# Warm-up matmuls, the spacing of the first block's bursts, and the place of one convolution in a tuned conv + SwiGLU kernel

## The chip, the cores and the metric

The kernel runs on one core of a Trainium2 chip. The metric is the device time of one execution in microseconds (us). "Span" is the time from the first to the last instruction of the profiled execution; in these runs it is 1.7 to 1.9 us shorter than the device time.

## The reference

```python
# x (8, 4096, 192), weight (8, 7); w_gate, w_val (192, 1536), w_out (1536, 192)
w   = softmax(weight)                       # seven taps for each of eight heads of 24 columns
y   = causal_conv_over_sequence(x, w)       # y[s] = sum_k w[h, k] * x[s - 6 + k]
y   = y.reshape(32768, 192)
out = (silu(y @ w_gate) * (y @ w_val)) @ w_out
```

## The kernel before

Tokens are worked through in 64 blocks of 512; a block has twelve *steps*. A step `n` computes one chunk of 128 hidden features: six matmuls of 512 columns for gate and value (`gate_val`), a silu on ScalarE, a product on VectorE. The down projection of the chunks is done in *bursts* of 12 or 24 matmuls (`slot(1)` to `slot(4)` for each block). Four blocks make a unit.

The convolution is done on TensorE too. For most units its result takes a detour ("the hop"): out to DRAM scratch and back through transposing DMAs. The first four blocks do not have time for all of that (in the kernel before, the first hop's writes and transposes are issued from 47.3 to 67.2 us, and the first gate matmul comes at 9.01 us): `early(e)` does their conv, and blocks 0 to 2 are turned by TensorE (`eturn`). The program divides PSUM into three "gate" banks, three "val" banks and two accumulators, which `eturn` and the conv borrow.

```python
    def keep_warm(count, width=TB):                      # TB = 512, P = 128
        for _ in range(count):
            seq(nc.tensor.matmul(warm[:, 0:width], fill[:, 0:P], fill[:, 0:width], ...))

    acc_banks = (apool, "acc0"), (apool, "acc1")
    keep_warm(7)
    spread_taps()          # two tiny matmuls, two VectorE operations
    keep_warm(5, P)
    make_wide()            # four matmuls of 256 columns, then copies out of PSUM
    early(0, (gate_bank, gate_bank, val_bank))
    eturn(0, (*acc_banks, gate_bank))
    make_band()

    for n in range(n_steps):
        b, j = divmod(n, NCH)                            # NCH = 12
        u, ls = divmod(n, ustep)                         # ustep = 48
        work = None
        if n in (11, 19):
            def work(e=2 if n == 11 else 3):
                early(e, (gate_bank, gate_bank, val_bank))
        at = (28, 31) if u == 0 else (10, 22)
        if u + 1 < NU and ls in at:
            def work(u=u, hh=at.index(ls)):
                conv_half(u + 1, hh)
        gate_val(n)
        if n == 5:
            early(1, (*acc_banks, gate_bank))
        elif n == 7:
            eturn(1, (*acc_banks, gate_bank))
        elif n in (9, 11):
            slot(1 if n == 9 else 2, b, silu[n - 1], work)
        elif n == 13:
            slot(3, 0, silu[n - 1])
        elif j % 3 == 1 and b:
            k = {1: 3, 4: 4, 7: 1, 10: 2}[j]
            slot(k, b - 1 if j < 7 else b, silu[n - 2], work if j > 4 else None)
            if j == 4 and work:
                work()
        if n == 18:
            eturn(2, (*acc_banks, gate_bank))
        # ... cut: writing out and fetching conv results, loads and copies of x
```

The third argument of `slot` is a silu that the burst must wait for. Bursts alternate which half of the array's rows adds into which accumulator, and the program takes the silu of a step as the sign that the burst before it has drained.

Of the kernel before, what the change touches and what calls it, by code (L numbers as in the profile page):

```python
# [10 lines left out]
def kernel(  # L11
# [9 lines left out]
    nc = tc.nc  # L21
    fp32 = mybir.dt.float32
    fp16 = mybir.dt.float16
# [11 lines left out]
    P = 128  # L35
# [4 lines left out]
    TB = P * SUBS  # L40
# [31 lines left out]
    def seq(i):  # L72

        e = i.ins.engine
        if e in last_on:
            tc.add_manual_dep(i.ins, last_on[e].name, NOSYNC, reason="order")
        last_on[e] = i.ins
        return i

    wpool = ctx.enter_context(tc.tile_pool(name="wts", bufs=1))  # L80
# [6 lines left out]

    wraw = wpool.tile([H, K], fp32, tag="wraw", name="wraw")
    seq(nc.sync.dma_start(out=wraw, in_=weight))
    fill = wpool.tile([P, TB], fp16, tag="fill", name="fill")  # L90
    seq(nc.vector.memset(fill, 0.0))  # L91


# [188 lines left out]
    def spread_taps():  # L282
        bank = apool.tile([P, TB], fp32, tag="acc0", name="tapbank")
        for a in range(2):
            seq(
                nc.tensor.matmul(
                    bank[:, a * H : a * H + H],
                    split[:, a].rearrange("h k q -> h (k q)"),
                    eye[0:H, 0:H],
                    start=(a == 0),  # L290
                    stop=True,
                    skip_group_check=True,
                )
            )
        seq(nc.vector.tensor_copy(tap, bank[:, 0 : 2 * H]))
        seq(
            nc.vector.tensor_tensor(
                spread.rearrange("p j a h -> p j (a h)"),
                eyes,
                tap.unsqueeze(1).to_broadcast([P, 16, 2 * H]),  # L300
                op=ALU.mult,
            )
        )
# [118 lines left out]
    def eturn(b, where):  # L422
        xc[b] = []
        for k in range(SL):
            t = cpool.tile([P, XW], fp16, tag=f"xc{k}", name=f"xc{k}", bufs=6)
            pool, tag = where[k]
            bank = pool.tile([P, EG, P], fp16, tag=tag, name="turn")
            for g in range(EG):
                seq(
                    nc.tensor.transpose(  # L430
                        bank[:, g, :], tme[b][:, g, Q * k : Q * k + P], ident
                    )
                )
            seq(
                (dve, act, dve)[k](
                    t.rearrange("p (g c j) -> p g c j", c=2, j=EO),
                    bank.rearrange("p g (c q) -> p g c q", c=2)[:, :, :, 0:EO],
                )
            )
            xc[b].append(t)  # L440
# [86 lines left out]
    silu = {}  # L527
# [26 lines left out]
    def down(b, work, swap, after):  # L554
        first = True
        for second, js in work:
            for j in js:
                hj = hbuf[b * NCH + j]
                for s in range(2):
                    for half in range(2):  # L560
                        bank = half ^ swap
                        p0 = Q * half
                        i = seq(
                            nc.tensor.matmul(  # L564
                                acc[b][bank][:, s, :],
                                hj[p0 : p0 + Q, ts(2 * bank + s, P)],
                                wo16[p0 : p0 + Q, j, :],
                                start=(not second and j == 0 and s == 0),
                                stop=(second and j == NCH - 1),
                                skip_group_check=True,  # L570
                            )
                        )
                        if first and after is not None:
                            tc.add_manual_dep(
                                i.ins, after.name, SYNC, reason="row halves swap banks"
                            )
                        first = False
                if second:
                    del hbuf[b * NCH + j]
# [15 lines left out]
    G = [range(3 * q, 3 * q + 3) for q in range(4)]  # L595

    def slot(k, b, after=None, between=None):

        if k == 1:
            acc[b] = [  # L600
                apool.tile([P, 2, D], fp32, tag=f"acc{i}", name=f"acc{i}")
                for i in range(2)
            ]
            down(b, [(False, G[0])], 1, after)
            if between is not None:
                between()
            down(b, [(False, G[1])], 1, None)
        elif k == 2:
            down(b, [(True, G[0]), (True, G[1])], 0, after)
            if between is not None:  # L610
                between()
            if b < n_blocks - 1:
                down(b, [(False, G[2])], 0, None)
        elif k == 3:
            down(b, [(True, G[2]), (False, G[3])], 1, after)
        else:
            down(b, [(True, G[3])], 0, after)
            o_sb = hpool.tile([P, SUBS, D], fp32, tag="o_sb", name="o_sb", bufs=3)
            seq(nc.scalar.copy(o_sb[:, 0:2, :], acc[b][0]))  # L619
            seq(nc.vector.tensor_copy(o_sb[:, 2:4, :], acc[b][1]))  # L620
            t0 = b * TB
            seq(
                nc.sync.dma_start(
                    out=out[t0 : t0 + TB, :].rearrange("(s p) d -> p s d", p=P),
                    in_=o_sb,
                )
            )
            del acc[b]


    warm = ppool.tile([P, TB], fp32, tag="gate", name="warm")

    def keep_warm(count, width=TB):
        for _ in range(count):
            seq(
                nc.tensor.matmul(  # L636
                    warm[:, 0:width], fill[:, 0:P], fill[:, 0:width],
                    start=True, stop=True, skip_group_check=True,
                )
            )  # L640

    gate_bank, val_bank = (ppool, "gate"), (ppool, "val")
    acc_banks = (apool, "acc0"), (apool, "acc1")
    keep_warm(7)
    spread_taps()
    keep_warm(5, P)
    make_wide()
    early(0, (gate_bank, gate_bank, val_bank))
    eturn(0, (*acc_banks, gate_bank))
# [3 lines left out]
    for n in range(n_steps):  # L653
        b, j = divmod(n, NCH)
        u, ls = divmod(n, ustep)
        work = None
        if n in (11, 19):

            def work(e=2 if n == 11 else 3):
                early(e, (gate_bank, gate_bank, val_bank))  # L660

        at = (28, 31) if u == 0 else (10, 22)
        if u + 1 < NU and ls in at:

            def work(u=u, hh=at.index(ls)):
# [4 lines that stand above are left out]
            early(1, (*acc_banks, gate_bank))  # L670
        elif n == 7:
            eturn(1, (*acc_banks, gate_bank))
        elif n in (9, 11):
            slot(1 if n == 9 else 2, b, silu[n - 1], work)
        elif n == 13:
            slot(3, 0, silu[n - 1])
        elif j % 3 == 1 and b:
            k = {1: 3, 4: 4, 7: 1, 10: 2}[j]
            slot(k, b - 1 if j < 7 else b, silu[n - 2], work if j > 4 else None)
            if j == 4 and work:  # L680
                work()
        if n == 18:
            eturn(2, (*acc_banks, gate_bank))
        elif n == 20:
            eout(3)
        elif n == 21:
            efetch(3)
        if u + 1 < NU:
            if ls == at[0]:
                conv_dup(u + 1)  # L690
            if ls == at[1]:
                for m in range(2):
                    conv_out(u + 1, m)
            if ls == at[1] + 1:
                for m in range(2, 8):
                    conv_out(u + 1, m)
            lo = 32 if u == 0 else 28
            if ls in range(lo, lo + 12, 3):
                fetch(UB * (u + 1) + (ls - lo) // 3)
        if u + 2 < NU:  # L700
            if ls == (22 if u == 0 else 1):
                x16_tile(u + 2)
                load_x(u + 2, 0, silu[n - 1])
            if ls == (25 if u == 0 else 5):
                load_x(u + 2, 1, silu[n - 1])
            if ls == (29 if u == 0 else 26):
                dup_x(u + 2)
    b = n_blocks - 1
    o_sb = hpool.tile([P, SUBS, D], fp32, tag="o_sb", name="o_sb", bufs=3)
    o_rows = out[b * TB : b * TB + TB, :].rearrange("(s p) d -> p s d", p=P)  # L710
# [5 lines left out]
    seq(nc.sync.dma_start(out=o_rows[:, 0:2, :], in_=o_sb[:, 0:2, :]))  # L716
    down_rows(b, 1, range(9, NCH))
    seq(nc.scalar.copy(o_sb[:, 2:4, :], acc[b][1]))  # L718
    seq(nc.scalar.dma_start(out=o_rows[:, 2:4, :], in_=o_sb[:, 2:4, :]))


# [28 lines left out]
```

## Time and profile before

| | before |
|---|---|
| device time, median of the first 3 runs | 793.12 us (792.34 to 794.83) |
| span of the profiled run | 790.9 us |
| TensorE busy | 783.5 us (99%) |
| VectorE, ScalarE busy | 582.9 us (74%), 522.1 us (66%) |
| chain that ended last | 97% TensorE |

From the page of the kernel before, the busy time of each engine and the chain that ended last, by engine:

```profile
PE 783.5 (99%) x12007; PEld 526.7 (67%) x12007; DVE 582.9 (74%) x928; ACT 522.1 (66%) x910; POOL 67.6 (9%) x95
...
PE 97%; POOL 1%; DMA 1%; DVE 0%; ACT 0%; issue 0%; POOLq 0%
```

TensorE is the limit, and in the long middle it has no gap (from 80 to 140 us it is busy for 60.0 of 60.0 us). So only the first 45 us and the last 5 can change. The timeline of TensorE in the kernel before, start of the kernel; the columns are start in us, duration in us, engine, line, operation, result and operands, shape and count, and in brackets the idle time before it with what ended it:

```profile
1.20 3.17 PE L636 MATMUL warm<-fill 128*128 128x512 f16 x7 [1.20 <-DVE fill L91]
4.31 0.21 PE L286 MATMUL tapbank<-eye,split 8*128 8x8 f16 x2
4.45 0.71 PE L636 MATMUL warm<-fill 128*128 128x128 f16 x5
5.11 1.01 PE L317 MATMUL taps<-spread,shift 128*128 128x256 f16 x4
6.68 0.82 PE L372 MATMUL cv<-xe,wide 64*64 64x72 f16 x64 [0.56 <-ACT wide L330]
8.01 1.04 PE L430 MATMUL turn<-ident,tme 128*128 128x128 f16 x15 [0.50 <-ACT tme L390]
```

Seven warm-ups begin at 1.20 us, and start every 0.427 us; later, matmuls of the same width start every 0.215 us. The trace records full clock from 6.21 us on. The rest is a chain with two pauses of 0.5 us. The first gate matmul follows at 9.01 us.

The same timeline at the last pair of step 9 and the first burst, which follows it, and around the first conv of unit 1 (step 28):

```profile
17.91 0.38 PE L538 MATMUL gate<-xc,w 64*128 64x512 f16 x1
17.91 0.38 PE L538 MATMUL val<-xc,w 64*128 64x512 f16 x1
18.32 1.16 PE L564 MATMUL acc<-wo,h 64*128 64x192 f16 x24
...
41.27 0.66 PE L564 MATMUL acc<-wo,h 64*128 64x192 f16 x12
41.86 0.73 PE L461 MATMUL cv<-x,band 64*32 64x240 f16 x32
42.52 0.40 PE L538 MATMUL gate<-xc,w 64*128 64x512 f16 x1
42.84 0.37 PE L538 MATMUL val<-xc,w 64*128 64x512 f16 x1
...
43.31 0.38 PE L538 MATMUL gate<-xc,w 64*128 64x512 f16 x1
43.87 0.37 PE L538 MATMUL val<-xc,w 64*128 64x512 f16 x1 [0.19 <-DVE tm L478]
```

Gate and value matmuls run as pairs, one in each half of the array, 0.215 us apart from pair to pair. The burst should start 0.21 us after the last pair and starts 0.41 us after it: a hidden wait of 0.2 us that no bracket shows, since a matmul's modelled end covers it (the records are 0.38 us long and start 0.215 us apart). After the conv the value matmuls fall 0.3 to 0.6 us behind their gates, because VectorE has not yet emptied the banks that the conv borrowed ("tm").

### The profile page before, as it was taken

How to read it: one execution, taken by the hardware profiler on the slowest of the kernel's cores; microseconds unless marked ns; L12 is line 12 of the kernel's file. 1: busy time of each engine (PE TensorE's matmuls, PEld its weight loads, DVE VectorE, ACT ScalarE, POOL GpSimd, SP SyncE). 2: the span in 40 equal slices, each digit the busy share in tenths (PEclk: the TensorE clock that was granted, in tenths of full speed). 3: DMA queues.
4: the chain of work that ended last, by engine and by line, in shares of the span. 5: the costliest groups of instructions: out<-in, count | busy, mean ns of one | idle time of the engine just before them, and what ended most of it. 6: DMA issues, size and time to landing. Idle time of an engine off the chain costs nothing.

```text
span 790.9 us, 28567 instructions
## 1 busy us (share of the span) xinstructions
PE 783.5 (99%) x12007; PEld 526.7 (67%) x12007; DVE 582.9 (74%) x928; ACT 522.1 (66%) x910; POOL 67.6 (9%) x95
## 2 busy tenths in 40 slices
PE   8999999999999999999999999999999999999997
PEld 5666666666666666666666666666666666666665
DVE  7677777777777777768777777777777777777775
ACT  6666666666666666766667666666667667676664
POOL 8101010010100101001010000100001010000000
PEclk9999999999999999999999999999999999999999
DMA  9999565787747778467894857857477784726211
GB/s 139 151 199 152 125 116 115 157 121 151 125 104 143 131 145 135 104 133 118 158 138 113 121 112 164 126 143 130 94 149 127 150 120 111 134 80 121 75 42 42
DMA packets 213825, 99.22 MB, mean 125 GB/s; under 512 B 147256, under 2 KB 212800, under 8 KB 212800
## 3 DMA queue, kind: packets, MB, share of 16 engines
q1 hardware_dynamic: 167424, 78.75, 47.4%
q0 software_dynamic: 46000, 18.45, 20.6%
q8 instruction: 94, 1.54, 0.8%
q14 instruction: 35, 0.29, 0.1%
q10 hardware_dynamic: 272, 0.20, 0.1%
HBM read 36.89 MB, written 41.16 MB: 99 GB/s over the span
## 4 chain that ended last, share of the span: by engine, by line
PE 97%; POOL 1%; DMA 1%; DVE 0%; ACT 0%; issue 0%; POOLq 0%
PE gate L538 61%; PE acc L564 32%; PE cv L461 2%; PE val L538 1%; DMA xe<-in_x_dram 1%; POOL w L167 0%; POOL xe L97 0%; PE acc L585 0%; PE cv L372 0%; PE turn L430 0%; DVE h L549 0%; ACT sig L547 0%; DVE tm L478 0%; ACT o_sb L718 0%; DVE o_sb L620 0%
## 5 line engine op out<-in xcount | busy, mean ns | idle before, releaser
L549 DVE TENSOR_TENSOR h<-sig,val 128x512 f16<-128x512 f16 x768 | 507.6, 688 | 195.8 <-PE val L538 194.3
L547 ACT ACTIVATE sig<-gate 128x512 f16<-128x512 f32 x768 | 458.6, 597 | 235.1 <-PE val L538 208.8
L538 PE MATMUL val<-xc,w 64*128 64x512 f16 x2304 | 539.2, 376 | 0.2 <-DVE tm L478 0.2
L538 PE MATMUL gate<-xc,w 64*128 64x512 f16 x2304 | 539.3, 376 | 0.0
L538 PEld LDWEIGHTS <-w 64*128 64x128 f16 x4608 | 254.0, 110 | 183.9 <-issue 1.6
L564 PEld LDWEIGHTS <-h 64*128 64x128 f16 x6096 | 257.4, 94 | 62.8 <-issue 6.1
L564 PE MATMUL acc<-wo,h 64*128 64x192 f16 x6096 | 298.8, 243 | 0.1
L97 POOL DMA_DIRECT2D x<-in_x_dram x40 | 31.5, 792 | 436.3 <-ACT sig L547 427.6
L478 ACT CAST tm<-cv 128x480 f16<-128x480 f32 x60 | 30.6, 562 | 22.0 <-PE cv L461 22.0
L478 DVE CAST tm<-cv 128x480 f16<-128x480 f32 x60 | 36.7, 653 | 2.6
L620 DVE COPY o_sb<-acc 128x384 f32<-128x384 f32 x63 | 34.7, 550 | 0.0
L489 POOL COPY tm<-tm 128x1280 f16<-128x1280 f16 x15 | 18.8, 1254 | 137.0 <-DVE tm L478 116.0
L619 ACT COPY o_sb<-acc 128x384 f32<-128x384 f32 x63 | 30.2, 480 | 0.0
L461 PE MATMUL cv<-x,band 64*32 64x240 f16 x960 | 18.2, 265 | 0.0
L461 PEld LDWEIGHTS <-band 64*32 64x32 f16 x960 | 10.1, 91 | 4.9 <-issue 4.7
L132 POOL MEMSET x<- 6x192 f16 x7 | 1.7, 248 | 59.7 <-PE cv L461 59.6
L97 POOL DMA_DIRECT2D xe<-in_x_dram x9 | 5.9, 672 | 0.8 <-DMA xe<-in_x_dram 0.6
L636 PE MATMUL warm<-fill 128*128 128x512 f16 (+1 forms) x12 | 3.9, 496 | 1.2 <-DVE fill L91 1.2
L390 ACT CAST tme<-cv 128x288 f16<-128x288 f32 x8 | 2.9, 401 | 2.6 <-PE cv L372 2.6
L372 PEld LDWEIGHTS <-wide 64*64 64x64 f16 x256 | 2.7, 108 | 2.0 <-ACT wide L330 1.0
L372 PE MATMUL cv<-xe,wide 64*64 64x72 f16 (+1 forms) x256 | 3.2, 192 | 0.7 <-ACT wide L330 0.6
L430 PE MATMUL turn<-ident,tme 128*128 128x128 f16 x45 | 3.1, 220 | 0.5 <-ACT tme L390 0.5
(52 smaller groups left out, 37.7 us busy)
## 6 DMA issues: line engine op xcount, KB each, us to landing
out_dram<-o_sb SPq DMA_DIRECT2D x63, 384.0 KB
scr<-tm SPq DMA_DIRECT2D x105, 130.0 KB
x<-x SPq DMA_DIRECT2D x28, 480.0 KB
x<-in_x_dram POOLq DMA_DIRECT2D x24, 480.0 KB, 9.0
x<-in_x_dram POOLq DMA_DIRECT2D x7, 468.0 KB, 7.1
xc<-scr SPq DMA_TRANSPOSE x180
scr<-tm SPq DMA_DIRECT2D x15, 104.0 KB
w<-in_moe_w_gate_dram POOLq DMA_DIRECT2D x3, 192.0 KB, 5.3
```

The lines of the kernel that those rows point to most:

```text
L97: nc.gpsimd.dma_start(out=t[p0 + i0 : p0 + i1, w0 - at : w1 - at, :], in_=bass.AP(tensor=x_flat.tensor, offset=(t0 + size * w0 - pad + i0) ...
L372: nc.tensor.matmul(o[Q * c : Q * c + Q, at : at + w], wide[Q * r : Q * r + Q, a, h, :], xe[e][Q * r : Q * r + Q, c : 2 * G : 2, h * grp : ...
L461: nc.tensor.matmul(banks[r][32 * c : 32 * c + 32, t * w : t * w + w], band[Q * r : Q * r + Q, h, :], x16[u][Q * r : Q * r + Q, NG * c : NG ...
L478: eng(tm[u][:, NG * r : NG * r + NG, 2 * grp * hp : 2 * grp * hp + 2 * grp].rearrange("p g (t e) -> p g t e", t=2), banks[r][:, 0 : 2 * w] ...
L489: seq(nc.gpsimd.tensor_copy(tm[u][:, :, SL * Q : 4 * Q], tm[u][:, :, 0:Q]))
L538: nc.tensor.matmul(o, w16[m][p0 : p0 + Q, k, e::E], xc[b][k][p0 : p0 + Q, 0:TB], start=(k == 0), stop=(k == SL - 1),)
L547: silu[n] = seq(nc.scalar.activation(sg, g, AF.Silu)).ins
L549: seq(nc.vector.tensor_tensor(hj, sg, v, op=ALU.mult))
L564: nc.tensor.matmul(acc[b][bank][:, s, :], hj[p0 : p0 + Q, ts(2 * bank + s, P)], wo16[p0 : p0 + Q, j, :], start=(not second and j == 0 and ...
L619: seq(nc.scalar.copy(o_sb[:, 0:2, :], acc[b][0]))
L620: seq(nc.vector.tensor_copy(o_sb[:, 2:4, :], acc[b][1]))
L636: nc.tensor.matmul(warm[:, 0:width], fill[:, 0:P], fill[:, 0:width], start=True, stop=True, skip_group_check=True,)
```

## The change

Its intent: keep TensorE busy from the first instruction until the taps, so that its clock rises early; give block 0's bursts the spacing of all later ones; put the first conv inside a burst, so that the banks it used are emptied during the rest of that burst; and move the copies of x out of the way of the hop. The diff, cut to its core:

```diff
-    fill = wpool.tile([P, TB], fp16, tag="fill", name="fill")
+    fill = wpool.tile([P, P], fp16, tag="fill", name="fill")
@@ slot, k == 3
-            down(b, [(True, G[2]), (False, G[3])], 1, after)
+            down(b, [(True, G[2])], 1, after)
+            if between is not None:
+                between()
+            down(b, [(False, G[3])], 1, None)
@@ start
-                    warm[:, 0:width], fill[:, 0:P], fill[:, 0:width],
+                    warm[:, 0:width], fill,
+                    fill.unsqueeze(1).to_broadcast([P, width // P, P]),
-    keep_warm(7)
+    keep_warm(8)
     spread_taps()
-    keep_warm(5, P)
+    keep_warm(4, 2 * P)
@@ steps
-        if n in (11, 19):
+        if n in (12, 19):                      # conv of block 2, of block 3
-        at = (28, 31) if u == 0 else (10, 22)
+        at = (25, 31) if u == 0 else (10, 22)
-        elif n in (9, 11):
-            slot(1 if n == 9 else 2, b, silu[n - 1], work)
-        elif n == 13:
-            slot(3, 0, silu[n - 1])
-        elif j % 3 == 1 and b:
+        elif n in (9, 12, 15, 17):
+            k = {9: 1, 12: 2, 15: 3, 17: 4}[n]
+            slot(k, 0, silu[n - 1 if k == 4 else n - 2], work)
+        elif j % 3 == 1 and n > 18:
-            slot(k, b - 1 if j < 7 else b, silu[n - 2], work if j > 4 else None)
-            if j == 4 and work:
-                work()
+            slot(k, b - 1 if j < 7 else b, silu[n - 2], work)
@@ loads and copies of x for unit 2 (steps 22, 25 and 29 become 21, 23 and 37)
-            if ls == (29 if u == 0 else 26):
+            if ls == (37 if u == 0 else 26):
                 dup_x(u + 2)
@@ last store
-    seq(nc.scalar.dma_start(out=o_rows[:, 2:4, :], in_=o_sb[:, 2:4, :]))
+    seq(nc.sync.dma_start(out=o_rows[:, 2:4, :], in_=o_sb[:, 2:4, :]))
```

More of the change, by code (lines that the diff above doesn't have):

```diff
@@ L656, with work @@
         work = None
-        if n in (11, 19):
-            def work(e=2 if n == 11 else 3):
+        if n in (12, 19):
+            def work(e=2 if n == 12 else 3):
                 early(e, (gate_bank, gate_bank, val_bank))
-        at = (28, 31) if u == 0 else (10, 22)
+        at = (25, 31) if u == 0 else (10, 22)
         if u + 1 < NU and ls in at:
@@ L700 @@
         if u + 2 < NU:
-            if ls == (22 if u == 0 else 1):
+            if ls == (21 if u == 0 else 1):
                 x16_tile(u + 2)
                 load_x(u + 2, 0, silu[n - 1])
-            if ls == (25 if u == 0 else 5):
+            if ls == (23 if u == 0 else 5):
                 load_x(u + 2, 1, silu[n - 1])
-            if ls == (29 if u == 0 else 26):
+            if ls == (37 if u == 0 else 26):
                 dup_x(u + 2)
```

## The prediction

> **What bounds the kernel now.** TensorE. The page has PE busy 783.5 of 790.9 us (99%), and the chain that ended last is 97% PE. From about 50 to 784 us the matmul timeline shows no idle time: a step of gate and value takes 0.645 us, twelve down matmuls 0.50. The change leaves those blocks alone, so only the 8 us before the first gate matmul, some stalls before 45 us and the 3.6 us after the last copy are in reach. ScalarE (66%) and VectorE (74%) have slack.
>
> **What it moves, costed from the matmul timeline.**
> 1. Down bursts of block 0. At 17.91, 20.41 and 24.17 us the burst starts 0.415 us after the last pair instead of 0.212: it waits for the silu of the step just before. Three steps apart and waiting for the silu two steps back, bursts 1 to 3 lose that: -0.6 us. Burst 4 moves from step 16 to 17 and waits for the step just before: +0.2. It now stands one step ahead of the transposes of block 2, which write the accumulator banks that its copies must empty. Before, VectorE's copy ended 1.5 us after the burst; the second transposes would now come about 1.1 us after it: +0.3 us stall.
> 2. First conv burst. At the end of a down burst, it makes gate/value wait for evacuation: pairs split at 42.52 to 43.88 us, and three steps take 2.47 us instead of 1.94. Inside a burst (as at 45.75 us) this vanishes: -0.5 us. x, issued by 19.3 us with at most 13.8 us to landing, is in time.
> 3. Start. Warm-up matmuls of 512 columns come every 427 ns, so the array is at half clock until about 6 us. [...] If the clock is released as late as in this trace, the extra matmul and the wider second group delay the taps (5.11 us) by 0.3 to 0.6 us. [...] On average -0.3 us.
> 4. Tail. ScalarE's store took about 2.2 us to land, SyncE's half 1.7: -0.2 us at most.
> 5. Copies of x later, loads slightly earlier: off the critical path, 0.
>
> Sum about -1.1 us, 0.14%.
>
> **Prediction.** 792.0 us, range 790.6 to 793.4. Faster by over 2%: 0.003; within 2%: 0.994; slower by over 2%: 0.003.
>
> **What would show each step.** Burst gaps of 0.21 us at steps 9, 12, 15, one of 0.41 at step 17; a pause of some 0.3 us within the transposes of step 18; no PE wait on "tm" after the first conv; warm-up spacing falling from 427 to 213 ns before the taps, and the first gate matmul at 8.2 to 9.3 us (now 9.01); steps from 50 us on unchanged; the end sooner after the last copy.
>
> **What would make it wrong.** [...]three runs span 2.5 us. Transfers of x colliding with unit 1's fetches so that PE waits for xc at step 48. A longer chain of bank waits around steps 17 to 19.

The terms of the forecast come to -0.1 (bursts), -0.5 (first conv), -0.3 (start) and -0.2 us (tail), together -1.1 us. "Phase" of the clock, where the recorded texts below use the word, is the time of its release, which differs from run to run: 4.76 to 6.21 us in six traces with the old start.

## The result, and the profile after

The changed kernel took 791.79 us (median of 4 runs, 791.17 to 793.09), the kernel before 793.04 us beside it (4 runs). The ratio is 0.9983, with a 95% interval of 0.9962 to 1.0004. Such a ratio is the mean time of one kernel's runs over that of the other's of the same rounds, so it is not quite the ratio of the medians. The predicted time of 792.0 us was 0.2 us off. The interval includes 1, so these eight runs alone do not show a gain; what was gained is read from the traces below.

From the page of the changed kernel, the busy times:

```profile
PE 782.5 (99%) x12007; PEld 526.3 (67%) x12007; DVE 583.0 (74%) x928; ACT 522.1 (66%) x910; POOL 67.6 (9%) x95
```

The timeline of TensorE in the changed kernel: the start, the conv of block 1, the burst of step 9, the burst of step 17 with the transposes of step 18, and the first conv of unit 1, now in step 25:

```profile
1.00 3.28 PE L639 MATMUL warm<-fill 128*128 128x512 f16 x8 [1.00 <-DVE fill L91]
4.22 0.20 PE L286 MATMUL tapbank<-eye,split 8*128 8x8 f16 x2
...
5.01 0.60 PE L317 MATMUL taps<-spread,shift 128*128 128x256 f16 x4
...
8.50 0.37 PE L538 MATMUL gate<-xc,w 64*128 64x512 f16 x1
...
12.75 0.38 PE L538 MATMUL val<-xc,w 64*128 64x512 f16 x1
13.56 1.03 PE L372 MATMUL cv<-xe,wide 64*64 64x72 f16 x64 [0.43 <-DMA xe<-in_x_dram]
14.52 0.40 PE L538 MATMUL gate<-xc,w 64*128 64x512 f16 x1
...
17.99 0.38 PE L538 MATMUL val<-xc,w 64*128 64x512 f16 x1
18.20 1.15 PE L564 MATMUL acc<-wo,h 64*128 64x192 f16 x24
...
27.41 0.38 PE L538 MATMUL val<-xc,w 64*128 64x512 f16 x1
27.82 0.67 PE L564 MATMUL acc<-wo,h 64*128 64x192 f16 x12
...
29.07 1.30 PE L430 MATMUL turn<-ident,tme 128*128 128x128 f16 x15
...
38.11 0.66 PE L564 MATMUL acc<-wo,h 64*128 64x192 f16 x12
38.70 0.73 PE L461 MATMUL cv<-x,band 64*32 64x240 f16 x32
39.36 0.67 PE L564 MATMUL acc<-wo,h 64*128 64x192 f16 x12
39.86 0.38 PE L538 MATMUL gate<-xc,w 64*128 64x512 f16 x1
39.86 0.38 PE L538 MATMUL val<-xc,w 64*128 64x512 f16 x1
```

Four things are to be seen. The burst of step 9 now starts 0.21 us after its last pair (17.99 to 18.20 us; the same at steps 12 and 15), and that of step 17 0.41 us after its own. In this run the clock rose early (at 3.84 us; the four matmuls for the taps take 0.60 us, not 1.01), and the first gate matmul came 0.5 us sooner. But the conv of block 1 then waited for the transfer of its x ("xe"), so that step 6, which begins right after it, began at 14.52 us against 14.44 before: this run kept nothing of its better start. The transposes of step 18 take 1.30 us where those of block 0 take 1.04: the new stall. And after the conv the gate and value matmuls stay together.

The last copy and the last store of the kernel before, from its timeline of ScalarE:

```profile
786.26 0.48 ACT L718 COPY o_sb<-acc 128x384 f32<-128x384 f32 x1 [1.65 <-PE acc L585]
786.77 0.41 ACTq L719 DMA_DIRECT2D out_dram<-o_sb  x1
```

The same in the changed kernel, where SyncE issues the store:

```profile
785.46 0.48 ACT L719 COPY o_sb<-acc 128x384 f32<-128x384 f32 x1 [1.65 <-PE acc L585]
786.05 0.39 SPq L720 DMA_DIRECT2D out_dram<-o_sb  x1
```

The traces allow an account by stretches between the same matmuls. "First gate of step n" is the start of that step's first gate matmul.

| stretch | before | after | difference |
|---|---|---|---|
| start to first gate of step 6 | 14.437 | 14.521 | +0.08 |
| to first gate of step 19 (bursts of block 0) | 15.918 | 15.784 | -0.13 |
| to step 23 (burst of step 19) | 6.045 | 5.861 | -0.18 |
| to step 48 (first conv of unit 1) | 26.198 | 25.633 | -0.57 |
| to ScalarE's last copy | 723.667 | 723.665 | 0 |
| last copy to the end of the span | 4.604 | 4.263 | -0.34 |

The sum is -1.14 us, the difference of the spans (790.869 and 789.727 us).

### The profile page after: what moved, and what is told of

Read it like the earlier page. It is cut to its first block, busy times and chain, and to the rows that moved or that the text cites. A ratio compares the mean times of both kernels' runs of the same rounds, so it can differ in the third digit from the quotient of the medians.

```text
span 789.7 us, 28564 instructions
## 1 busy us (share of the span) xinstructions
PE 782.5 (99%) x12007; PEld 526.3 (67%) x12007; DVE 583.0 (74%) x928; ACT 522.1 (66%) x910; POOL 67.6 (9%) x95
## 4 chain that ended last, share of the span: by engine, by line
PE 97%; POOL 1%; DMA 1%; DVE 0%; ACT 0%; issue 0%; POOLq 0%
PE gate L538 61%; PE acc L564 32%; PE cv L461 2%; PE val L538 1%; DMA xe<-in_x_dram 1%; POOL w L167 0%; POOL xe L97 0%; PE acc L585 0%; PE cv L372 0%; PE turn L430 0%; DVE h L549 0%; ACT sig L547 0%; DVE o_sb L623 0%; ACT o_sb L719 0%; POOL jn L191 0%
## 5 line engine op out<-in xcount | busy, mean ns | idle before, releaser
L372 PE MATMUL cv<-xe,wide 64*64 64x48 f16 (+1 forms) x256 | 3.2, 192 | 1.1 <-ACT wide L330 0.6
```

The lines of the kernel that those rows point to most:

```text
L372: nc.tensor.matmul(o[Q * c : Q * c + Q, at : at + w], wide[Q * r : Q * r + Q, a, h, :], xe[e][Q * r : Q * r + Q, c : 2 * G : 2, h * grp : ...
```

## The experiments

A single look (one run and its trace) cannot measure 0.5 us by its time, so most verdicts come from the stretches of its trace. The theory after the first comparison: the bursts, the conv and the tail make the gain, and whatever the start wins is lost again at step 5, where the conv of block 1 waits for xe. The rival: the start counts in full, and the clock decides it.

### One part of the change at a time

e1_start: the kernel before with the start alone (this edit and some of the next are cut to their core).

```diff
-    keep_warm(7)          # and fill of 512 columns
+    keep_warm(8)          # and fill of 128 columns, repeated as operand
     spread_taps()
-    keep_warm(5, P)
+    keep_warm(4, 2 * P)
```

> The kernel before with the start alone changed (fill of 128 columns, eight warm-ups, four of 256). Theory (the landing of block 1's x, xe, gates step 5's conv): the first gate matmul moves with the clock's release, to about 8.5 us if released near 3.8 us and up to 9.3 us if later, but the first gate matmul after the conv of block 1 stays at 14.4 to 14.6 us, PE waits 0.3 to 0.8 us for the transfer of xe, and the span from there to the end is that of before within 0.2 us. Rival (the start's gain is kept): that matmul comes as much earlier as the first gate one did, 13.9 to 14.0 us.

Measured: release of the clock at 4.18 us (the trace records when the granted clock changes), first gate at 8.66 us, and step 6 at 13.79 us, with no wait for xe. The theory fails, and step 6 comes even sooner than the rival's 13.9 to 14.0 us. Of the 0.64 us against the kernel before, 0.35 us are the earlier first gate; the other 0.30 us are the wait at step 5 that the trace of the kernel before has and this one has not (see the table below). So the landing of xe is no fixed wall. One time, 792.60 us, beside 792.38 of the kernel before; its trace has a pause of 0.4 us in the burst after step 202 for which it names no releaser; more on those below.

e2_bursts: the kernel before with the steps 9, 12, 15, 17 alone (cut: the conv of block 2 goes to step 12, as in the change).

```diff
-        elif n in (9, 11): slot(1 if n == 9 else 2, b, silu[n - 1], work)
-        elif n == 13:      slot(3, 0, silu[n - 1])
-        elif j % 3 == 1 and b:
+        elif n in (9, 12, 15, 17):
+            k = {9: 1, 12: 2, 15: 3, 17: 4}[n]
+            slot(k, 0, silu[n - 1 if k == 4 else n - 2], work)
+        elif j % 3 == 1 and n > 18:
```

> The kernel before with block 0's bursts alone moved (steps 9, 12, 15, 17, conv of block 2 at 12). Theory: bursts at 9, 12, 15 follow the last pair by 0.21 us, that at 17 by 0.41, the transposes of step 18 pause 0.35 us, and from the first gate of step 6 to the first of step 19 it takes 15.8 us against 15.92 before, so three removed waits of 0.2 us give only 0.1 to 0.2 us; the burst of step 19 no longer takes 0.19 us extra, so some 0.3 us by step 22. Rival (the waits removed are all won): 0.6 us.

Measured: 15.785 us from step 6 to step 19 (before 15.918) and 5.862 from there to step 23 (before 6.045), so 0.32 us in all, as the theory had it. One time, 792.36 us.

e3_conv: the first conv alone, inside step 25's burst instead of after step 28's; the loads and copies of x stay where they were (cut: the split of `slot(3)` and its call with `work`, as in the change).

```diff
-        at = (28, 31) if u == 0 else (10, 22)
+        at = (25, 31) if u == 0 else (10, 22)
```

> The kernel before with the first conv burst of unit 1 alone moved from the end of step 28's burst into that of step 25. Theory: no split of gate from val after it, the burst of step 34 comes 0.55 us sooner after that of step 22 (13.26 us against 13.82). Rival (x not landed by step 25, or the evacuation delays step 26 instead): less than 0.3 us won, with a PE wait on x or tm.

Measured: 13.26 us from step 23 to step 35, against 13.82 before: -0.56, as expected. But then the trace has a wait that neither side of this expectation names in this place; the prediction has it, PE waiting for xc at step 48, among what would make it wrong. The waits of TensorE in e3_conv (engine, line, what it waited for, total us, times, longest):

```profile
PE gate L538 <- DMA xc<-scr: 0.6, 1, 0.6
PE acc L564 <- issue: 0.3, 1, 0.3
```

Step 48, the first one that is fed through the hop, lasts 0.91 us longer. The timeline of SyncE's queue shows why. First that of e3_conv (start in us, us until the last of the group was issued, queue, line, operation, result and source):

```profile
44.23 5.47 SPq L147 DMA_DIRECT2D x<-x  x2
49.78 6.99 SPq L497 DMA_DIRECT2D scr<-tm  x8
57.23 12.37 SPq L519 DMA_TRANSPOSE xc<-scr  x9
```

Then that of the changed kernel, where the copies `x<-x` come behind the first transposes:

```profile
46.37 5.73 SPq L497 DMA_DIRECT2D scr<-tm  x8
52.64 7.81 SPq L519 DMA_TRANSPOSE xc<-scr  x6
60.56 2.20 SPq L147 DMA_DIRECT2D x<-x  x2
```

In e3_conv, GpSimd's copy for the conv now stands in its queue ahead of the second load of x, which is issued at 41.9 us (before: 38.8). SyncE waits 4.3 us for it, with the hop's writes queued behind: the transposes begin at 57.2 us, against 54.7 in the kernel before and 52.6 in the changed kernel. The earlier loads and the copies after the hop are thus not idle housekeeping (no run moves only one of the two); without them the moved conv lost more at step 48 of this run than it had won. One time, 793.25 us.

e4_tail: the last store from SyncE instead of ScalarE.

```diff
-    seq(nc.scalar.dma_start(out=o_rows[:, 2:4, :], in_=o_sb[:, 2:4, :]))
+    seq(nc.sync.dma_start(out=o_rows[:, 2:4, :], in_=o_sb[:, 2:4, :]))
```

> The kernel before with the last store alone issued from SyncE. Theory: from the start of ScalarE's last copy to the end of the span 4.2 us against 4.60 before, nothing else moves. Rival (the tail differs by chance, or both halves on one queue land one after the other): 4.5 us or more.

Measured: 4.15 us from the start of the last copy to the end. In all, seven traces with the old store (the kernel before, e1_start, e2_bursts, e3_conv, both looks at the kernel before and f3_pause) have 4.60 to 4.80 us there, mean 4.66, and seven with the new one 4.15 to 4.30, mean 4.25. The tail is worth 0.41 us. By the packets, ScalarE's store ended 2.25 us after its issue began (786.77 to 789.02 us in the kernel before), SyncE's 1.75 us (786.05 to 787.80 us in the changed kernel). One time, 791.91 us.

### The start, the clock and the transfer of xe

e6_late_early: the changed kernel with conv and transposes of block 1 one step later.

```diff
-        if n == 5:
+        if n == 6:
             early(1, (*acc_banks, gate_bank))
-        elif n == 7:
+        elif n == 8:
             eturn(1, (*acc_banks, gate_bank))
```

> The changed kernel with the conv of block 1 at step 6 instead of 5 and its transposes at step 8 instead of 7. Theory (xe lands near 13.5 to 13.9 us and step 5's conv waits for it): PE no longer waits there, or under 0.3 us, and the start's gain comes through: the first gate of step 19 comes 0.4 to 0.8 us sooner than the 30.31 us of the changed kernel, unless the burst of step 9 waits for banks of the transposes (up to 0.3 us). Time about 791.2 us. Rival (something else holds step 5): no gain.

Measured: no wait for xe, but no gain: step 19 begins at 30.66 us (changed kernel: 30.31 and 30.54), and the median is 791.86 us (6 runs) beside 791.80 (4 runs) of the changed kernel. In this run the clock came at 6.33 us and the first gate at 9.54 us, so xe would have been nearly there in any case; from step 9 to step 12 it took 3.09 us instead of 2.93, probably since the burst of step 9 now comes right behind the transposes. The expectation failed: the wait of 0.8 us in the first trace was an unusually long one.

after_again: the changed kernel, unaltered.

> The changed kernel unaltered, for a second look at the clock's phase and the run to run spread. Theory: [...]the first gate after block 1's conv is again at 14.4 to 14.6 us. Rival: this matmul follows the first gate matmul at a fixed distance of 6.0 us.

Measured: 791.80 us (median of 4 runs, 791.50 to 792.60), ratio 0.9983 (0.9965 to 1.0000). Release at 6.49 us, first gate at 9.54 us, step 6 at 14.75 us. From the first gate to step 6 it takes 5.21 us here, 6.02 in the first trace and 5.13 in e1_start; the distance is not fixed, as the rival wanted, and step 6 is not fixed either.

e8_cold: the changed kernel without warm-ups.

```diff
-    keep_warm(8)
     spread_taps()
-    keep_warm(4, 2 * P)
```

> The changed kernel without any warm-up matmuls. Theory: the clock is released late (after 7 us), the first gate matmul comes at 9.3 us or later against 8.50, but the first gate after block 1's conv at most 0.5 us later than 14.52, because that waits for xe anyway; the span grows by under 0.6 us. Rival (the start is on the critical path in full, clock phase explains runs 2.5 us apart): that matmul and the span are 1 us or more later.

Measured: release at 12.57 us, first gate at 9.45 us, step 6 at 15.90 us, ScalarE's last copy at 786.89 us (changed kernel: 785.46 and 785.70). One time, 792.98 us. The theory allowed 0.5 us at step 6 and it is 1.15 to 1.4 us: it falls, and the start is on the critical path nearly in full. Note the first gate: with no warm-up at all it comes no later than in the changed kernel with a late clock (9.54 us). What a late clock costs is the steps after it: the first pairs start 0.41 us apart here (9.45 and 9.86 us), where those after a release start 0.215 us apart.

The starts together, of the kernels that do the same up to step 6; "wait" is what the time from step 5 to step 6 exceeds 1.58 us, the least seen (the traces of the kernel before, before_look1, e2_bursts and after name the transfer of xe as the releaser of a matmul or of its weight load, after 0.21, 0.23, 0.17 and 0.43 us of idle time; for the 0.52 us of before_look2 the answers name no transfer of xe, and for the three smaller waits no releaser is named):

| trace | start | clock released | first gate | step 6 | wait for xe |
|---|---|---|---|---|---|
| before | old | 6.21 | 9.01 | 14.44 | 0.30 |
| before_look1 | old | 4.76 | 8.59 | 14.15 | 0.43 |
| before_look2 | old | 5.86 | 8.95 | 14.60 | 0.52 |
| e2_bursts | old | 5.48 | 8.92 | 14.35 | 0.37 |
| e3_conv | old | 5.47 | 8.92 | 13.98 | 0 |
| e4_tail | old | 5.65 | 8.92 | 14.17 | 0.19 |
| after | new | 3.84 | 8.50 | 14.52 | 0.80 |
| after_again | new | 6.49 | 9.54 | 14.75 | 0.15 |
| e1_start | new | 4.18 | 8.66 | 13.79 | 0 |
| e7_turn_banks | new | 4.87 | 8.93 | 14.08 | 0.09 |

(e6_late_early and f2_best do other things there and e8_cold and f3_pause have starts of their own.) The mean of step 6 is 14.28 us with the old start and 14.29 us with the new one: in these looks the new start wins nothing. But six and four looks, whose step 6 spreads over 0.6 and 1.0 us, cannot tell 0 from the predicted -0.3 us. For a given release it even delays the first gate (4.87 us gives 8.93, where the old start had 8.59 at 4.76), since the taps wait for the longer warm-up (they begin at 5.50 us in after_again, at 5.11 in the kernel before). Its use may be elsewhere.

### The runs near 795 us

In the end the kernel before had 36 timed runs. They fall into two groups: 27 from 791.93 to 793.89 us, and 9 from 794.76 to 795.69 us. Of 21 runs of kernels with the new start (after, after_again, e1_start, e6_late_early, e7_turn_banks, f2_best) none is over 793.09 us. If the group had nothing to do with the kernel, none of 21 would come about once in a hundred times (an estimate from 9 of 57). But of the 21 only the one of e1_start has the start without the rest of the change, so these counts alone do not say which part removes the group. Two more looks were to catch such a run in a trace.

> The kernel before unaltered, in search of one of its runs near 795 us (4 of the 15 timed so far are over 794.5, none of 14 of kernels with the new start). Theory A[...]: such a run shows a release after 9 us and its first gate after block 1's conv 1 us or more later than 14.4; a run near 793 shows a release between 5 and 6.5 us. Theory B: such a run shows a release before 7 us and its loss elsewhere, as pauses in the later steps.

> As before_look1: the same kernel once more, with the same two theories and numbers.

(Theory A puts such a run down to a late release of the clock; the way in which it has pauses delay the release is cut here and under f3_pause, as no trace shows it.)

Measured: 793.39 and 792.84 us. Neither is of the upper group, so these two looks do not decide. (The releases, 4.76 and 5.86 us, are not both in the 5 to 6.5 us of theory A.) The first shows another kind of loss: in a burst at 218.5 us TensorE starts nothing for 1.0 us, and its waits name no releaser (columns as for e3_conv):

```profile
PE acc L564 <- issue: 0.8, 1, 0.8
```

Pauses like this, which add 0.4 to 0.9 us, appear in four of the fourteen traces (e1_start, e3_conv, f2_best and before_look1), after steps 202, 637, 61 and 202. What causes them was not shown: the traces name no releaser, and no experiment here tested it.

f3_pause: the kernel before with a longer pause at the taps.

```diff
     spread_taps()
-    keep_warm(5, P)
     make_wide()
```

> The kernel before without its five warm-ups of 128 columns, so that TensorE pauses longer between the taps' two groups. So far 6 of 26 runs of the kernel before are over 794.5 us and none of 21 with the new start. Theory A[...]: at least half of these runs are over 794.5 us, and the profiled one, if it is such, shows the release after 9 us and first gate after block 1's conv 1 us or more later than 14.4. Theory B (the slow runs come from later pauses and have nothing to do with the start): the share stays near a quarter, and a profiled slow run shows its loss after step 20.

Measured: 793.38, 795.28, 796.98, 795.75 and 796.46 us: four of five are over 794.5 us. The ratio is 1.0034 (1.0019 to 1.0050) to the kernel before, which had three of nine runs in the upper group. So with a pause of 0.6 us at the taps, filled until then, such long runs are the rule, and three are longer than any of the kernel before. The profiled run was the one of 793.38 us, the fastest, and even this one shows the clock lost again. Busy times by stretches in f3_pause (stretch, its length, busy us and instructions of TensorE, its weight loads, VectorE, ScalarE and GpSimd, then the granted clock, DMA share and GB/s); the first runs from the release to the next recorded change, the second is from another answer:

```profile
4.36:7.78 3.41, 1.76 (x74) 1.33 (x73) 2.04 (x7) 1.42 (x4) 3.41 (x7) 1.00 1.04 136
...
8.00:11.00 3.00, 3.00 (x22) 1.91 (x22) 0.95 (x3) 0.91 (x2) 2.16 (x4) 0.50 1.10 146
```

(The view shows full clock ahead of the first change, for which it has no record; the warm-ups start 0.427 us apart there.) The clock was released at 4.36 us, and in the 3.41 us after it TensorE was busy for 1.76 us only. At 7.78 us the clock went back to half (0.50 in the second line, where matmul pairs of 512 columns start 0.43 us apart), and it was released again at 11.19 us (0.215 us apart from 11.25 us on). No single pause between 4.36 and 7.78 us was longer than 0.6 us: they are 0.59, 0.56 and 0.50 us.

In a stretch of the same length after the first release TensorE was busy for 2.28 us or more in all other traces (2.28 in before_look1, 2.55 in the changed kernel's), and these kept the clock (their mean granted clock over the span is 0.999 or 1.000, that of this run of f3_pause 0.997). That the difference in busy time is what lost it in f3_pause was not tried. The old start has pauses of 0.56 and 0.50 us behind its taps. That they have to do with the upper group of the unaltered kernel before is supported by f3_pause, in which one more pause, of 0.59 us, raises the share of runs over 794.5 us from a quarter to four of five. How they would is not shown: the changed kernel has pauses of 0.56 and 0.50 us in the same places, and no such run. But no trace of a run over 794.5 us was caught, of either kernel, and losing the clock once is not enough to explain such a run: the profiled run of f3_pause lost it once, reached step 6 at 15.08 us, 0.64 us later than the kernel before, and is of the lower group. The two groups are 2.1 us apart in the mean. What such a run does in detail stays open.

### The stall of step 18, and a version without it

e7_turn_banks: the changed kernel, transposes of block 2 into other banks.

```diff
-            eturn(2, (*acc_banks, gate_bank))
+            eturn(2, (gate_bank, val_bank, gate_bank))
```

> The changed kernel with the transposes of block 2 (step 18) in gate and val banks instead of the accumulators'. Theory (their pause of 0.35 us is the wait for VectorE's copy of block 0's second accumulator): the pause is gone; the gate and value matmuls of steps 19 or 20 may wait for those banks instead, so the burst of step 22 moves by -0.35 to +0.3 us. Rival (the pause is of the weights or of tme): it stays in the transposes.

Measured: the transposes of step 18 without the pause, in the timeline of e7_turn_banks:

```profile
28.63 1.01 PE L430 MATMUL turn<-ident,tme 128*128 128x128 f16 x15
29.57 0.40 PE L538 MATMUL gate<-xc,w 64*128 64x512 f16 x1
```

From step 16 to step 19 it takes 3.69 us instead of 3.98, and from there to step 23 5.86 us, as before. So 0.29 us are won and kept: the stall was the wait for the accumulator's copy. One time, 790.74 us, under every run of the changed kernel so far.

f2_best: this, and a start with a shorter warm-up ahead of the taps and some more behind them.

```diff
-    keep_warm(8)
+    keep_warm(7)
     spread_taps()
-    keep_warm(4, 2 * P)
+    keep_warm(3, 2 * P)
     make_wide()
+    keep_warm(4, P)
@@
-            eturn(2, (*acc_banks, gate_bank))
+            eturn(2, (gate_bank, val_bank, gate_bank))
```

> The changed kernel with the transposes of block 2 in gate and val banks, seven warm-ups of 512 columns, three of 256, and four of 128 in the pause before the first conv. Theory: the pause of step 18 stays away (from the first gate of step 16 to that of step 19 3.69 us), the first gate matmul comes by 9.0 us even where the clock is released after 6 us (9.54 with eight and four), no run over 793 us; median 790.7 to 791.3, below both kernels. Rival (the start is settled by the transfer of xe alone): the start gives nothing and the median is 791.4 or more.

Measured: 790.94 us (median of 5 runs, 790.68 to 792.42), ratio to the kernel before 0.9967 (0.9951 to 0.9983), a gain clear of noise though far from 2%. With the clock released at 5.88 us the first gate came at 8.92 us, as hoped. The profiled run was its slowest: the second half of xe landed 1.0 us late there, and a pause of 0.7 us without a releaser came at 76 us. The conv of block 1 in f2_best:

```profile
13.31 0.22 PE L372 MATMUL cv<-xe,wide 64*64 64x72 f16 x1
14.32 0.72 PE L372 MATMUL cv<-xe,wide 64*64 64x48 f16 x63 [0.79 <-DMA xe<-in_x_dram]
```

It was not timed in the same rounds as the changed kernel; the medians differ by 0.86 us. Which share of it the start has is not separated from that of the banks.

## Why the prediction was right, point by point

The time was right (792.0 predicted, 791.79 measured) and so was the class. That it was only 0.2 us off is in part luck: four runs of a kernel lie 1.9 us and more apart, and the terms of the sum were not all right; what it put too low in the tail and at step 19 (0.2 us each) about makes up for what the looks do not show of the start.

1. **Bursts of block 0: predicted -0.6 + 0.2 + 0.3 = -0.1 us; measured -0.13 us, and -0.18 us more at step 19.** The three gaps fell to 0.21 us, step 17 has one of 0.41 us, and the transposes of step 18 pause (0.29 us by e7_turn_banks). What the prediction missed is that the burst of step 19 took 0.18 us extra before and does not any more (e2_bursts shows both parts).
2. **First conv: predicted -0.5 us; measured -0.57 us** (e3_conv: -0.56 us).
3. **Start: predicted -0.3 us on average; measured nothing in the looks, which cannot exclude it.** This is the step that the runs do not bear out. The late case was rightly sized: with a late clock (6.49 us) the first gate came at 9.54 us, 0.5 us later than before. With an early one (3.84 us) it came at 8.50 us, 0.5 us sooner. But in the four looks early clocks are not common enough to move the average of step 6, and in the first trace even the early clock was lost to the wait for xe, which the prediction had not seen. What the new start may buy is something else: the runs near 795 us (9 of 36) are gone (0 of 21), though that the start did it is not shown. Without them the mean of the kernel before is 0.5 us lower (793.48 with those runs, 792.96 without them), its median hardly. So over all its runs an average of -0.3 us for the start may yet be right; it stays open.
4. **Tail: predicted -0.2 us at most; measured -0.41 us** over seven traces each. That the store from SyncE ends sooner was right, its size half of the truth; the prediction's own landing times, 2.2 and 1.7 us, already differed by 0.5 us. Issuing took 0.41 us on ScalarE and 0.39 us on SyncE, so it is not that. It was ScalarE's only transfer; whether that is the cause was not tried.
5. **Copies of x: predicted 0; measured 0 as part of the whole.** But "off the critical path" holds only of the whole: with the conv moved and loads and copies left alone, step 48 waited 0.91 us (e3_conv). They are a condition of point 2.

The stretches that differ alike in all traces sum to -0.13 - 0.18 - 0.57 - 0.41 = -1.29 us, and the medians differ by 1.25 us. So these four, each shown by an experiment of its own, carry the gain between the medians.

## What to carry to other kernels

When one engine is 99% busy, look for its waits in the distance from one start to the next, not only in the listed idle time: the waits of 0.2 us in the bursts were in no list. Put work that borrows banks in the middle of other work of the same engine (-0.57 us here), and when you move a producer earlier, ask which queues its helpers stand in; here the move paid only together with the moved loads and copies. And where the clock of TensorE is not the same in every run (here it was released at 3.84 us in one run of the changed kernel and at 6.49 us in another, and lost again in one of f3_pause), count the runs by groups before believing a mean: filling a pause may leave the usual run as it is, and still take away the bad ones (here f3_pause speaks for it, but it was not shown).
